# Softmax sums inverted on 128x7 through DRAM, and banks emptied whole, in a fused attention and expert kernel

## The chip, the cores and the metric

The kernel runs on one core of a Trainium2 chip. The metric is the device time of one execution in microseconds, from the profiler's clock; the times of three runs are given by their median.

## The reference

An attention over 2 batches, 12 heads, 448 positions and 64 features per head, with capped scores, feeds two expert blocks that work on 896 tokens of 768 features. The expert weights come as 64-bit floats.

```python
scores = scale * np.matmul(q, k.transpose(0, 1, 3, 2))
scores = cap * np.tanh(scores / cap)
scores = scores - np.max(scores, axis=-1, keepdims=True)
attn = np.exp(scores)
attn = attn / (np.sum(attn, axis=-1, keepdims=True) + 1e-09)
attn_out = np.matmul(attn, v)
x = attn_out.transpose(0, 2, 1, 3).reshape(896, 768)
xn = x / np.sqrt(np.mean(x * x, axis=-1, keepdims=True) + 1e-06) * rms_g
g = xn @ w_gate
x = g * (1.0 / (1.0 + np.exp(-g))) * (xn @ w_val) @ w_out
return ((x @ w1) * (x @ w2) @ w3) @ w_out2
```

## The kernel before, in words

The program has two stages. The **attention** works through 12 pairs of heads (`NP`); features lie on partitions. For a pair the keys are cut into chunks of 128, the last half chunks of the two heads together, which makes 42 groups (`NG`). A group is scores on PE (`scores`, line 440: three matmuls per head, on operands split into a high and a low half), tanh and exp on ACT over two banks at once (lines 448 and 454, into the tile `t`), and the values product on PE (`pv`, line 471), which accumulates a head's bank `po`. There are two `po` banks, one per head of a pair. Each head's values stand beside 64 columns of ones, so a bank holds 64 rows of unnormalized values and 64 rows that all equal the softmax sum.

When a pair's last chunk is accumulated, four steps empty its two banks: for each head `take_sum` (lines 482 and 484) copies the 64 rows of sums plus a small guard into half of the tile `sm`, and `take` (lines 180 and 182) copies the 64 rows of values into the tile `xraw`. Then `invert` takes the reciprocal of `sm` in two steps of 128 x 224 on DVE (line 499), `normalize` multiplies `xraw` by it (line 507, DVE or POOL), `square` (line 518, ACT) and `add_square` (line 525) build the sum of squares for the expert block's norm.

```python
def invert(pr, c):
    def run(e):
        r = sums[pr][:, c * S // 2 : (c + 1) * S // 2]
        e.reciprocal(r, r)
```

Into the attention's gaps on PE goes half of the product of the last two weight matrices (`last_product`, lines 642 to 644), whose result waits in DRAM (`m32`). The 64-bit weights are loaded as raw words (`wraw`), rebuilt on POOL, ACT and DVE (lines 264 to 281) and split in two halves (`wo`, `whl`; lines 180 to 187).

The **expert** stage (`experts`, matmuls at lines 791 to 793) is a list of weight tiles, each used for both batches; the first four tiles run for batch 0 before any runs for batch 1, whose norm comes last (`normalize_x`, lines 315 to 330).

What sets the order of the work is a planner (class `Plan`). Every step is a task with its engines and an assumed duration on each, a rank, the tasks it comes after, and the buffers of fixed rings (`rings`) that it makes and uses. `order` plays the tasks through once, and the program is issued in that order: each engine, SP's queue of DMA issues included, works in its own part of it strictly in order and waits wherever the real times differ from the assumed ones. All DMAs of the program are issued by SP.

## Time and profile before

| what | value |
|---|---|
| median of three runs | 644.07 us (643.78 to 645.33) |
| the profiled execution | 644.65 us |
| its span, first to last instruction | 642.5 us |
| attention, first tanh to last exp | 6.86 to 138.19 us |
| first expert matmul | 159.05 us |

The span is a little shorter than the time of the execution, since the launch and the end lie around it. The page names each engine's share of the whole span; as the two stages differ, the views by stretch say more. PE is the matmul engine (TensorE), PEld its weight loads, DVE VectorE, ACT ScalarE, POOL GpSimd, SP the engine that issues the DMAs.

### The profile page before, as it was taken

Reading aid. Unit: us, or ns where it says so; the run is one execution under the profiler, and the core shown is the slowest. Engines: PE = TensorE matmul, PEld = TensorE weight load, DVE = VectorE, ACT = ScalarE, POOL = GpSimd, SP = SyncE. Lnnn points to the kernel's source line nnn. Section 1 sums busy time; section 2 is a strip of 40 time slices with the busy share of each in tenths; the row PEclk is TensorE's granted clock in tenths of the full one; section 3 lists DMA queues with packets and bytes.
Section 4 is the critical chain, followed back from the end, with each engine's and each line's share of the span. In section 5 each row is a group of like instructions: output and inputs, shape, how many; then the busy total and the mean of one; then the engine's idle time right before and its main releaser. Section 6 shows DMA issues by size and latency. Waiting matters only on the chain.

```text
span 642.5 us, 7766 instructions
## 1 busy us (share of the span) xinstructions
PE 625.0 (97%) x2985; PEld 529.0 (82%) x2985; DVE 390.0 (61%) x474; ACT 277.2 (43%) x383; POOL 162.8 (25%) x161
## 2 busy tenths in 40 slices
PE   6899999999999999999999999999999999999996
PEld 2455556669999999999999999999999999999995
DVE  2898999979867677524765555576565564332300
ACT  6798788965434344223433332233332232121111
POOL 1747532213133344222422222211132221000000
PEclk9899999999999999999999999999999999999999
DMA  8554542325345444225863222333222332224411
GB/s 313 171 201 142 186 142 78 112 73 185 112 153 186 138 141 153 93 71 187 258 211 99 98 99 99 107 129 107 99 99 98 99 118 96 66 65 142 141 46 47
DMA packets 33886, 82.91 MB, mean 129 GB/s; under 512 B 2992, under 2 KB 21040, under 8 KB 33840
## 3 DMA queue, kind: packets, MB, share of 16 engines
q1 hardware_dynamic: 33840, 82.33, 38.4%
q8 instruction: 25, 0.41, 0.3%
q14 instruction: 21, 0.17, 0.1%
HBM read 73.27 MB, written 9.04 MB: 128 GB/s over the span
## 4 chain that ended last, share of the span: by engine, by line
PE 82%; DVE 9%; ACT 5%; issue 2%; POOL 1%; DMA 1%; SPq 0%; ACTq 0%; POOLq 0%; DVEq 0%
PE bank L791 25%; PE bank L793 25%; PE bank L792 25%; PE po L471 3%; DVE sm L499 3%; PE pss L440 2%; ACT t L448 1%; DVE wraw L277 1%; ACT t L454 1%; DVE wraw L281 1%; DVE th L187 1%; PE bank L642 1%; POOL xraw L507 1%; PE bank L644 1%; PE bank L643 1%
## 5 line engine op out<-in xcount | busy, mean ns | idle before, releaser
L273 POOL TENSOR_SCALAR wraw<-wraw 128x768 int32<-128x768 uint32 (+1 forms) x71 | 77.6, 1093 | 195.0 <-DMA wraw<-in_w 85.2
L187 DVE TENSOR_TENSOR whl<-wraw,whl 128x768 fp32r<-128x768 f32 (+1 forms) x80 | 70.1, 876 | 79.5 <-POOL whl L184 65.4
L791 PE MATMUL bank<-xn,whl 128*128 128x448 f32 x288 | 105.6, 367 | 0.5 <-POOL wraw L273 0.5
L792 PE MATMUL bank<-xn,whl 128*128 128x448 f32 x288 | 105.6, 367 | 0.0
L793 PE MATMUL bank<-xn,whl 128*128 128x448 f32 x288 | 105.6, 367 | 0.0
L277 DVE SCALAR_TENSOR_TENSOR wraw<-wraw 128x768 int32<-128x768 int32 (+1 forms) x76 | 70.7, 931 | 48.8 <-POOL wraw L273 43.8
L184 POOL TENSOR_SCALAR whl<-wraw 128x768 fp32r<-128x768 f32 (+1 forms) x47 | 42.4, 902 | 202.0 <-PE bank L793 160.8
L281 DVE SCALAR_TENSOR_TENSOR wraw<-wraw 128x768 int32<-128x768 int32 (+1 forms) x76 | 79.2, 1042 | 1.7
L791 PE MATMUL bank<-u,whl 128*128 128x448 f32 x216 | 79.3, 367 | 0.0
L793 PE MATMUL bank<-u,whl 128*128 128x448 f32 x216 | 79.3, 367 | 0.0
L792 PE MATMUL bank<-u,whl 128*128 128x448 f32 x216 | 79.3, 367 | 0.0
L471 PE MATMUL po<-t,v 128*128 128x448 f32 (+1 forms) x192 | 75.1, 566 | 2.6 <-DVE xraw L182 1.4
L264 ACT ACTIVATE wraw<-wraw 128x768 f32<-128x768 f32 (+1 forms) x59 | 52.1, 882 | 45.8 <-DMA wraw<-in_wgv 16.3
L791 PE MATMUL bank<-y,whl 128*128 128x448 f32 x192 | 70.7, 368 | 0.0
L792 PE MATMUL bank<-y,whl 128*128 128x448 f32 x192 | 70.7, 368 | 0.0
L793 PE MATMUL bank<-y,whl 128*128 128x448 f32 x192 | 70.7, 368 | 0.0
L471 PEld LDWEIGHTS po<-t,v 128*128 128x128 f32 (+1 forms) x192 | 31.5, 192 | 33.5 <-issue 25.4
L791 PEld LDWEIGHTS bank<-xn,whl 128*128 128x128 f32 x288 | 54.1, 188 | 5.7 <-POOL wraw L273 0.8
L793 PEld LDWEIGHTS bank<-xn,whl 128*128 128x128 f32 x288 | 54.1, 188 | 4.9
L792 PEld LDWEIGHTS bank<-xn,whl 128*128 128x128 f32 x288 | 54.1, 188 | 4.7
L180 ACT ACTIVATE whl<-wraw 128x768 fp32r<-128x768 f32 (+1 forms) x33 | 28.3, 858 | 42.2 <-PE bank L793 40.6
L448 ACT ACTIVATE t<-pss,small 128x896 f32<-128x896 f32 x42 | 41.9, 998 | 10.3 <-PE pss L440 8.4
(89 smaller groups left out, 938.8 us busy)
## 6 DMA issues: line engine op xcount, KB each, us to landing
wraw<-in_wgv SPq DMA_DIRECT2D x24, 768.0 KB, 4.4
wraw<-in_w SPq DMA_DIRECT2D x16, 768.0 KB, 4.2
wraw<-in_wdn SPq DMA_DIRECT2D x12, 768.0 KB, 4.2
wraw<-in_w3t SPq DMA_DIRECT2D x16, 512.0 KB, 3.9
wraw<-in_wo SPq DMA_DIRECT2D x8, 768.0 KB, 6.7
m<-mo SPq DMA_DIRECT2D x32, 192.0 KB, 2.7
wraw<-m SPq DMA_DIRECT2D x24, 256.0 KB, 3.2
v<-in_v SPq DMA_DIRECT2D x12, 448.0 KB, 3.8
```

The source lines that it names most:

```text
L180: nc.scalar.activation(out_, in_, AF.Copy)
L184: nc.gpsimd.tensor_scalar(out_, in_, 1.0, 1.0, op0=ALU.mult, op1=ALU.mult)
L187: e.tensor_tensor(lo, raw, r32(hi), op=ALU.subtract)
L264: e.activation(h, h, AF.Copy, scale=2.0**-112)
L273: e.tensor_scalar(l, l.bitcast(U32), 0.876 * 2.0**-29, 0.49, op0=ALU.mult, op1=ALU.add)
L277: e.scalar_tensor_tensor(l, h, 3, l, op0=ALU.logical_shift_left, op1=ALU.bitwise_or)
L281: e.scalar_tensor_tensor(l, h, -(2**31), l, op0=ALU.bitwise_and, op1=ALU.bitwise_or)
L448: e.activation(chunks[g], s[:, :, :S], AF.Tanh, scale=tsc)
L471: e.matmul(pos[2 * p + i][:, :S], vals[p][rows, 6 if c == 3 else 2 * c + i, :], x, start=start, stop=stop)
L791: e.matmul(dst, whi[:, c, :], src(0, g, b), start=(g == 0), stop=False)
L792: e.matmul(dst, whi[:, c, :], src(1, g, b), start=False, stop=False)
L793: e.matmul(dst, wlo[:, c, :], src(0, g, b), start=False, stop=(g == total - 1))
```

## The change

Each `po` bank is emptied by one copy of all 128 rows into a new tile `ev` (a ring of four, two pairs). The second head of a pair now has its ones ahead of its values, so its values come out on partitions 64 to 127, where they are wanted. For the first ten pairs one row of sums of each head goes to DRAM (`keep`, into `total`), comes back as 128 x 7 (`gather`, tile `rs`), gets its guard and its reciprocal on DVE (`invert`), goes out again (`put`, into `rcp`) and comes back spread over 64 partitions per head (`spread`, tile `rb`). For the last two pairs the sums are stacked on 128 partitions and inverted as before (`stack`, `invert_stacked`). `normalize` works on 64 rows of one head at a time, from `ev` into `xraw`. The rings of values (`v`), of exponentials (`t`), raw weights (`raw`) and product copies (`mo`) are one deeper. The planner knows a fixed time to landing for the new transfers (`lands`) and a slack for SP's steps behind other engines; the second half of `wo` lies in a pool that is opened when the attention's is closed. The other branch of the program, for large caps, is not run with these inputs.

```diff
-NRAW, NHL, EARLY = 3, 4, 4
+NRAW, NHL, EARLY = 4, 4, 4
...
+    SLACK = 1.5
...
-                if (self.tasks[j]["on"].keys() == {self.tasks[i]["e"]}) == same:
+                on = self.tasks[j]["on"].keys()
+                if (0 if on == {self.tasks[i]["e"]} else 2 if on == {"SP"} else 1) == for_:
                     missing[j] -= 1
...
-                end = [free[e], free[e] + self.LAG[e]]
+                end = [free[e], free[e] + self.LAG[e], free[e] + self.SLACK]
                 if t["size"]:
                     channel = max(channel, now + 1.5) + t["size"] / self.RATE
-                    end = [channel + 0.5] * 2
+                    end = [channel + 0.5] * 3
+                if t["lands"]:
+                    end = [now + t["lands"]] * 3
...
+    total = dram.tile([HP, 2 * S], F32, name="total")
+    rcp = dram.tile([HP, 2 * S], F32, name="rcp")
...
-        rings = dict(qk=2, th=3, v=3, t=4, sm=2, sq=2, s=2, o=2, m=2, raw=NRAW, hl=NHL, mo=2, sg=4, acc=2)
+        rings = dict(qk=2, th=3, v=4, t=5, ev=4, rs=2, rb=3, sq=2, s=2, o=2, m=2, raw=NRAW, hl=NHL, mo=3, sg=4, acc=2)
...
-            def take_sum(i):
-                def run(e):
-                    pr, j = divmod(i, 2)
+            def take(i):
+
+
+                def run(e):
+                    taken[i] = ring(ap, "ev", [P, S])
+                    half(taken[i], pos[i][:, :S], e)
+
+                return run
+
+            def stack(pr, j):
+                def run(e):
                     if j == 0:
-                        sums[pr] = ring(ap, "sm", [P, S])
-                    s = slice(j * D, (j + 1) * D)
+                        inv_[pr] = ring(ap, "rb", [P, S])
+                    r, at = slice(j * D, (j + 1) * D), slice((1 - j) * D, (2 - j) * D)
                     if e is nc.scalar:
-                        e.activation(sums[pr][s], pos[i][D:, :S], AF.Identity, bias=guard[D:])
+                        e.activation(inv_[pr][r], taken[2 * pr + j][at], AF.Identity, bias=guard[at])
                     else:
-                        e.tensor_scalar(sums[pr][s], pos[i][D:, :S], guard[D:], None, op0=ALU.add)
-
-                return run
-
-            def take(i):
+                        e.tensor_scalar(inv_[pr][r], taken[2 * pr + j][at], guard[at], None, op0=ALU.add)
...
+            def invert_stacked(pr, c):
+                def run(e):
+                    r = inv_[pr][:, c * S // 2 : (c + 1) * S // 2]
+                    e.reciprocal(r, r)
...
+            def keep(pr):
+                def run(e):
+                    for j in range(2):
+                        at = D * (1 - j)
+                        e.dma_start(out=total[pr : pr + 1, j * S : (j + 1) * S], in_=taken[2 * pr + j][at : at + 1])
...
+            def gather(pr):
+                def run(e):
+                    rows_[pr] = ring(ap, "rs", [P, 2 * S // P])
+                    e.dma_start(out=rows_[pr], in_=total[pr].rearrange("(p n) -> p n", p=P))
...
+            def invert(pr):
+                def run(e):
+                    e.tensor_scalar(rows_[pr], rows_[pr], guard, None, op0=ALU.add)
+                    e.reciprocal(rows_[pr], rows_[pr])
...
+            def put(pr):
+                def run(e):
+                    e.dma_start(out=rcp[pr].rearrange("(p n) -> p n", p=P), in_=rows_[pr])
+
...
+            def spread(pr):
+                def run(e):
+                    inv_[pr] = ring(ap, "rb", [P, S])
+                    for j in range(2):
+                        e.dma_start(out=inv_[pr][j * D : (j + 1) * D], in_=rcp[pr : pr + 1, j * S : (j + 1) * S].to_broadcast([D, S]))
...
+            def normalize(i):
                 def run(e):
                     pr, j = divmod(i, 2)
                     b, h = divmod(pr, H // 2)
-                    half(x_tile(b, h)[j * D : (j + 1) * D], pos[i][:D, :S], e)
-
...
-            def invert(pr, c):
-                def run(e):
-                    r = sums[pr][:, c * S // 2 : (c + 1) * S // 2]
-                    e.reciprocal(r, r)
...
-            def normalize(pr):
-                def run(e):
-                    b, h = divmod(pr, H // 2)
-                    x = xraw[b][:, h, :]
-                    e.tensor_tensor(x, x, sums[pr], op=ALU.mult)
+                    r = slice(j * D, (j + 1) * D)
+                    e.tensor_tensor(x_tile(b, h)[r], taken[i][r], inv_[pr][r], op=ALU.mult)
...
+                    ev = [evb[2 * p], evb[2 * p + 1]]
+                    done = [add(dict(ACT=0.57, DVE=0.66), take(2 * p + i), r - 2 + i * 0.01, after=[a], makes=[ev[i]], uses=[both[i]]) for i in range(2)]
+                    if p >= NP - 2:
+                        a = [add(dict(ACT=0.66, DVE=0.66), stack(p, 0), r, after=[done[0]], makes=[rbb[p]], uses=[ev[0]])]
+                        a.append(add(dict(ACT=0.66, DVE=0.66), stack(p, 1), r, after=[done[1], a[0]], uses=[ev[1], rbb[p]]))
+                        inv = [add(("DVE", 1.52), invert_stacked(p, c), r + 0.1 * c, after=a, uses=[rbb[p]]) for c in range(2)]
+                    else:
+                        a = add(("SP", 0.9), keep(p), r - 30, after=done, uses=ev, lands=3.2)
+                        a = add(("SP", 0.45), gather(p), r - 30, after=[a], makes=[rsb[p]], lands=2.8)
+                        a = add(("DVE", 0.35), invert(p), r - 30, after=[a], uses=[rsb[p]])
+                        a = add(("SP", 0.45), put(p), r - 30, after=[a], uses=[rsb[p]], lands=3.0)
+                        inv = [add(("SP", 0.9), spread(p), r - 30, after=[a], makes=[rbb[p]], lands=4.0)]
                     done = []
                     for i in range(2):
-                        done.append(add(dict(ACT=0.66, DVE=0.66), take_sum(2 * p + i), r - 2 + i * 0.01, after=[a] + done[:1],
-                                        makes=[] if i else [smb[p]], uses=[both[i]] + ([smb[p]] if i else [])))
                         new = b not in x_alloc
-                        x = add(dict(ACT=0.57, DVE=0.66), take(2 * p + i), r - 2 + 0.1 + i * 0.01, after=[a] + ([] if new else [x_alloc[b]]),
-                                makes=[xb[b]] if new else [], uses=[both[i]] + ([] if new else [xb[b]]))
+                        x = add(dict(DVE=0.66) if h == 5 else dict(DVE=0.66, POOL=1.3), normalize(2 * p + i), r + 0.3 + 0.01 * i,
+                                after=inv + ([] if new else [x_alloc[b]]), makes=[xb[b]] if new else [], uses=[rbb[p], ev[i]] + ([] if new else [xb[b]]))
                         x_alloc.setdefault(b, x)
                         done.append(x)
-                    inv = [add(("DVE", 1.52), invert(p, c), r + 0.1 * c, after=done, uses=[smb[p]]) for c in range(2)]
-                    a = add(dict(DVE=0.66) if h == 5 else dict(DVE=0.66, POOL=1.3), normalize(p), r + 0.3, after=inv, uses=[smb[p], xb[b]])
-                    every.append(a)
-                    a = add(("ACT", 0.58), square(p), r + 0.4, after=[a], makes=[sqb[p]] if h else [], uses=[xb[b]])
+                    a = add(("ACT", 0.58), square(p), r + 0.4, after=done, makes=[sqb[p]] if h else [], uses=[xb[b]])
                     if h:
                         a = add(dict(DVE=0.66) if h == 5 else dict(DVE=0.66, POOL=1.3), add_square(p), r + 0.5, after=[a, sq_last[b]], uses=[sqb[p]])
                     sq_last[b] = a
...
+                        wo[q] = ring(up() if q else big, "BC"[q], [P, 2, HJ, DM], F32R, "wo")
...
+                                 ready=[done[0][0]] if r else over))
...
-    v = np.concatenate([a["v"].reshape(BH, S, D), np.ones((BH, S, D), np.float32)], axis=2).reshape(BH // 2, 2, S, P)
+    v = a["v"].reshape(BH // 2, 2, S, D)
+    ones = np.ones((BH // 2, S, D), np.float32)
+    v = np.stack([np.concatenate([v[:, 0], ones], axis=2), np.concatenate([ones, v[:, 1]], axis=2)], axis=1)
```

Since the planner decides the order, the built order shows more than the diff. On PE, at the end of the first pair and the start of the second (`pss` is a bank pair of scores, `po` the values product), before and with the change:

```order
5 L471 MATMUL po<-t,v 128x448 x2
6 L440 MATMUL pss<-th 128x448 x6
7 L471 MATMUL po<-t,v 128x448 x2
8 L440 MATMUL pss<-th 128x448 x6
9 L471 MATMUL po<-t,v 128x448 x6
10 L440 MATMUL pss<-th 128x448 x12
11 L471 MATMUL po<-t,v 128x448 x2
```

```order
5 L478 MATMUL po<-t,v 128x448 x2
6 L447 MATMUL pss<-th 128x448 x6
7 L478 MATMUL po<-t,v 128x448 x2
8 L447 MATMUL pss<-th 128x448 x6
9 L478 MATMUL po<-t,v 128x448 x8
10 L447 MATMUL pss<-th 128x448 x18
11 L697 MATMUL bank<-wo,whl 128x384
```

One more values product of the second pair comes ahead of the next scores, and three groups of scores then stand in a row. Further on, 102 matmuls of the last product stand behind the last values product, where 93 did.

On DVE, from the first emptied bank on (`sm` sums, `th` split heads, `ev` emptied banks, `rs` the 128 x 7 sums), before and with the change:

```order
13 L182 COPY xraw<-po 64x448
14 L484 TENSOR_SCALAR sm<-po,small 64x448
15 L277 SCALAR_TENSOR_TENSOR wraw<-wraw 128x768
16 L499 RECIPROCAL sm<-sm 128x224
17 L187 TENSOR_TENSOR th<-qk,th 128x960
18 L499 RECIPROCAL sm<-sm 128x224
19 L187 TENSOR_TENSOR th<-qk,th 128x960
```

```order
13 L188 COPY ev<-po 128x448
14 L283 SCALAR_TENSOR_TENSOR wraw<-wraw 128x768
15 L287 SCALAR_TENSOR_TENSOR wraw<-wraw 128x768
16 L283 SCALAR_TENSOR_TENSOR wraw<-wraw 128x768
17 L287 SCALAR_TENSOR_TENSOR wraw<-wraw 128x768
18 L193 TENSOR_TENSOR th<-qk,th 128x960
19 L283 SCALAR_TENSOR_TENSOR wraw<-wraw 128x512
20 L287 SCALAR_TENSOR_TENSOR wraw<-wraw 128x512
21 L193 TENSOR_TENSOR wo<-wraw,wo 128x768
22 L188 COPY ev<-po 128x448
23 L531 TENSOR_SCALAR rs<-rs,small 128x7
24 L532 RECIPROCAL rs<-rs 128x7
```

The wide reciprocals are gone, weight steps stand in their place, and the first pair's small reciprocal comes after the second pair's first bank copy.

On SP, the transfers of the first two pairs among the loads, with the change, after the first pair's sums have gone out (`total` and `rcp` lie in DRAM, `rb` takes the spread reciprocals):

```order
18 L525 DMA rs<-total 128x7
19 L407 DMA qk<-in_qk 128x960
20 L431 DMA v<-in_v 128x896
21 L257 DMA wraw<-in_w3t 128x1024
22 L516 DMA total<-ev 1x448 x2
23 L538 DMA rcp<-rs 128x7
24 L407 DMA qk<-in_qk 128x960
25 L257 DMA wraw<-in_w3t 128x1024 x2
26 L525 DMA rs<-total 128x7
27 L546 DMA rb<-rcp 64x448 x2
```

Between two steps of one pair stand loads of heads, values and weights, and the steps of the next pair.

## Rows read from the trace of the kernel before

**Rows 1.** The page, busy share (part 1) and granted clock by slice (part 2).

```profile
PE 625.0 (97%) x2985; PEld 529.0 (82%) x2985; DVE 390.0 (61%) x474; ACT 277.2 (43%) x383; POOL 162.8 (25%) x161
...
PEclk9899999999999999999999999999999999999999
```

**Rows 2.** Busy us (count) of PE, PEld, DVE, ACT, POOL by stretch; clock, DMA share, GB/s.

```profile
6.86:137.20 130.34, 124.44 (x523) 70.61 (x522) 113.89 (x121) 112.90 (x135) 55.63 (x52) 0.99 0.46 158
...
159.05:642.50 483.45, 477.34 (x2352) 438.75 (x2352) 255.67 (x324) 151.08 (x229) 100.89 (x97) 1.00 0.36 119
```

**Rows 3.** ACT's groups, 6.86 to 137.2 us: busy, mean ns, idle before.

```profile
L454 ACT ACTIVATE t<-t,small 128x896 f32<-128x896 f32 x42 | 43.7, 1041 | 1.1
L448 ACT ACTIVATE t<-pss,small 128x896 f32<-128x896 f32 x42 | 41.9, 998 | 10.3 <-PE pss L440 8.4 <-PE po L471 1.6
L482 ACT ACTIVATE sm<-po,small 64x448 f32<-64x448 f32 x12 | 7.6, 632 | 0.4
L180 ACT ACTIVATE xraw<-po 64x448 f32<-64x448 f32 x12 | 6.5, 538 | 2.5 <-DVE sm L484 2.3
L518 ACT ACTIVATE sq<-xraw 128x448 f32<-128x448 f32 x8 | 4.6, 575 | 4.9 <-POOL xraw L507 3.1 <-DVE xraw L507 1.7
...
L271 ACT ACTIVATE wraw<-wraw 128x768 int32<-128x768 uint32 (+1 forms) x3 | 2.5, 822 | 0.3 <-DMA wraw<-in_w3t 0.3
...
L180 ACT ACTIVATE mo<-bank 128x384 f32<-128x384 f32 x2 | 0.9, 472 | 0.0
```

**Rows 4.** DVE's groups by shape, 0 to 158 us.

```profile
L499 DVE RECIPROCAL sm<-sm 128x224 f32<-128x224 f32 x24 | 35.7, 1524 | 0.2
...
L484 DVE TENSOR_SCALAR sm<-po,small 64x448 f32<-64x448 f32 x11 | 7.6, 690 | 3.3 <-PE po L471 1.8 <-ACT xraw L180 1.2
...
L182 DVE COPY xraw<-po 64x448 f32<-64x448 f32 x11 | 6.8, 615 | 2.0 <-ACT sm L482 1.8
...
L507 DVE TENSOR_TENSOR xraw<-xraw,sm 128x448 f32<-128x448 f32 x7 | 5.3, 758 | 0.1
...
L200 DVE TENSOR_TENSOR small<-small 128x1 f32<-128x1 f32 x1 | 0.2, 159 | 0.0
```

**Rows 5.** Timeline at the attention's end: start, us, engine, instruction, idle before.

```profile
137.15 1.04 ACT L454 ACTIVATE t<-t,small 128x896 f32<-128x896 f32 x1
...
141.14 0.68 PE L642 MATMUL bank<-wo,whl 128*128 128x384 f32 x1
...
157.70 0.33 PE L644 MATMUL bank<-wo,whl 128*128 128x384 f32 x1
...
158.22 0.34 PE L644 MATMUL bank<-wo,whl 128*128 128x384 f32 x1
159.05 0.44 PE L791 MATMUL bank<-xn,whl 128*128 128x448 f32 x1 [0.49 <-POOL wraw L273]
```

**Rows 6.** POOL's group of line 507, 0 to 158 us.

```profile
L507 POOL TENSOR_TENSOR xraw<-xraw,sm 128x448 f32<-128x448 f32 x5 | 9.3, 1856 | 15.7 <-DVE sm L499 11.8 <-ACT t L448 3.9
```

**Rows 7.** DMA issues up to 150 us (KB, us to landing), then the tile m.

```profile
m<-mo SPq DMA_DIRECT2D x11, 192.0 KB, 1.9
...
small<-in_rg SPq DMA_DIRECT2D x1, 3.0 KB, 5.5
...
L613 SPq DMA_DIRECT2D m<-mo x32: 319/320/931, 71.5 to 326.0; - x32
...
DMA to landing us min/median/max: 1.8/3.1/4.7
```

**Rows 8.** The tile sm: min/median/max ns, first and last start.

```profile
L482 ACT ACTIVATE sm<-po,small x13: 629/632/635, 19.0 to 140.9; 64x448 f32<-64x448 f32 x13
```

**Rows 9.** Who PE waited for: total us, times, longest.

```profile
PE po L471 <- DVE xraw L182: 1.4, 2, 0.8
```

**Rows 10.** Busy time by stretch, two stretches near the start.

```profile
21.60:24.00 2.40, 2.40 (x5) 1.15 (x6) 2.40 (x3) 2.40 (x3) 1.41 (x1) 0.79 0.53 214
24.00:27.00 3.00, 3.00 (x6) 1.31 (x5) 3.00 (x3) 1.43 (x2) 0.75 (x1) 0.60 0.43 111
```

More of the change, by code (lines that the diff above doesn't have):

```diff
@@ L70, in buf, with add @@
         return b
-    def add(self, engines, run, rank, after=(), makes=(), uses=(), size=0, behind=()):
+    def add(self, engines, run, rank, after=(), makes=(), uses=(), size=0, behind=(), lands=0):
         if not isinstance(engines, dict):
@@ L81, in add @@
         self.tasks.append(
-            dict(on=engines, run=run, rank=rank, after=[x for x in after if x is not None], makes=list(makes), held=held, size=size, behind=list(behind))
+            dict(on=engines, run=run, rank=rank, after=[x for x in after if x is not None], makes=list(makes), held=held, size=size, behind=list(behind), lands=lands)
         )
@@ L142, in order @@
                 todo -= 1
-                ends += [(end[0], i, True), (end[1], i, False)]
+                ends += [(x, i, k) for k, x in enumerate(end)]
                 moved = True
@@ L152, in order @@
                 finish(*x[1:])
-                if not x[2]:
+                if x[2] == 1:
                     for h in self.tasks[x[1]]["held"]:
@@ L375, in attend @@
             NP = BH // 2
-            raws, heads, vals, chunks, pos, sums, sqs = {}, {}, {}, {}, {}, {}, {}
+            raws, heads, vals, chunks, pos, taken, rows_, inv_, sqs = {}, {}, {}, {}, {}, {}, {}, {}, {}
             qkb, thb = {p: buf("qk") for p in range(1, NP)}, {p: buf("th") for p in range(NP)}
             vb, tb, ob = {p: buf("v") for p in range(NP)}, {g: buf("t") for g in range(NG)}, {i: buf("o") for i in range(BH)}
-            smb, sqb = {p: buf("sm") for p in range(NP)}, {p: buf("sq") for p in range(NP)}
+            evb, rsb = {i: buf("ev") for i in range(BH)}, {p: buf("rs") for p in range(NP)}
+            rbb, sqb = {p: buf("rb") for p in range(NP)}, {p: buf("sq") for p in range(NP)}
             first_of = lambda p: 7 * (p // 2) + 3 * (p % 2)
@@ L585, in layer, with prep_wo @@
         wo_done, wob = {}, [buf("B", -1), buf("C", -1)]
-        def prep_wo(q, rank, when, step):
+        def prep_wo(q, rank, when, step, over=()):
             done = wo_done[q] = []
@@ L704, in attend_any @@
                 for k in range(NK):
-                    nc.tensor.matmul(po, tv[:, order[k], :D], pt[:, k, :], start=(k == 0), stop=(k == NK - 1))
+                    nc.tensor.matmul(po, tv[:, order[k], rows], pt[:, k, :], start=(k == 0), stop=(k == NK - 1))
                 x = x_tile(b, h)
@@ L738, in experts @@
             at = [t[0] for t in seq].index("prod")
-            prep_wo(1, 2000 + 10 * (at - 8.5), 60 + at - 8.5, 2)
+            prep_wo(1, 2000 + 10 * (at - 8.5), 60 + at - 8.5, 2, over)
             def get_w(k):
```

11 lines of the change are left out of this document (7 added, 4 removed).

## The prediction

> **What bounds the kernel now.** Start with the page: PE is busy in 97% of the span and its granted clock is full in nearly every slice [rows 1], which reads like a kernel that nothing off PE can help. That figure is an average over two different stages, so the next view is busy time by stretch [rows 2]. From 159.05 us on the expert layers run: PE is busy 477 of 483 us, DVE 256, ACT 151, and the change issues the same matmuls there. Nothing is to be had in that stage. In the attention, from the first tanh at 6.86 us to the last one's stretch at 137.2, the other engines are nearly full too: of 130.3 us DVE is busy 113.9, ACT 112.9, POOL 55.6. PE shows 124.4, but a modelled end covers the start of a wait, so this is not PE at its peak.
>
> Who sets the pace in the attention? Every chunk goes scores (PE), tanh, exp (ACT), values product (PE). ACT's groups [rows 3] say what it does in those 130 us: 84 tanh and exp are 85.6 us, which nobody can take from it; the banks' emptying (sums 7.6, values 6.5) is 14.1. Its idle time is mostly waits for PE's scores (8.4), which in turn stand behind bank waits on PE, and 2.3 in front of L180, which waits for DVE's half of the same emptying. DVE's groups [rows 4] show where the time goes that the change aims at: 24 reciprocals of 1.52 us are 35.7 us. The end of the attention is in the timeline [rows 5]: last exp from 137.15 to 138.19, last values product done before 141.14, then 93 matmuls of the second product and the sums' matmul up to 158.22, then the experts. So whatever ends the last exp earlier moves the whole expert stage, less what PE still has to do in between.
>
> **The change, part by part.** *ACT up to the last exp*, counted in the built order. Twelve sums go (12 x 0.632 = -7.6 us); twelve value copies of 64 rows become ten bank copies of 128 rows by 448, at the same 448 elements per partition and so at the same 0.538 (-1.1); one square less (-0.6), two product copies go to DVE (-0.9), one weight step goes and two come (+0.8 at 0.82 each) [rows 3]. Sum: -9.4 us.
>
> *DVE.* Away: 20 of 24 reciprocals (-30.5), 11 sums (-7.6), 11 copies (-6.8), 7 normalizings (-5.3). Added: 12 bank copies at 0.615 (+7.4), 17 normalizings of 64 x 448 at the old mean of 0.758 (+12.9), twenty steps on 128 x 7, nearest to the 128 x 1 steps at 0.16 (+3.2), some 3 for additions and copies that move over [rows 4]. Net about -24 us of 114. DVE does not set the end, so I give this nothing directly; it is the cover under the next two items.
>
> *POOL* normalizes 7 times instead of 5. Each took 1.856 us [rows 6], against DVE's mean of 0.758, and ACT's squares wait behind it: 3.1 us for five [rows 3]. Two more: +1.2 us of waiting on ACT.
>
> *Waits.* The wait of 2.3 in front of ACT's L180 goes, since a bank now has one reader that waits for PE alone. New waits come: DVE stops in order at the small reciprocal (for the gathered row) and at the normalizing (for the spread one), and behind it stand the next pair's head split (L187), weight steps and bank copies. The trace of before has no such wait. Below, the cost can be nothing: DVE has 16 us idle already and 24 more, over ten pairs 2.4 us each beyond what it has. Above it is the 11 us of the first rival. I take 2.3, the wait that they replace, because the transfers' nearest row is close to its short end (below). The two entries cancel.
>
> *The transfers.* Ten pairs make six each, 60 in all, with four landings in a row: sums out, gathered, reciprocals out, spread. The nearest ones are the stores `m<-mo`: 1.9 us median to landing in the attention, 1.8 to 4.7 over the run, 0.32 of SP to issue [rows 7]. At 1.9 the path from the emptied bank is 2.2 + 2.2 + 0.3 + 2.2 + 2.5 and two normalizings at 0.61, 10.7 us. The banks' copies have a ring of four, so pair p+2 may overwrite when pair p is normalized. Pairs end 11.1 us apart (19.0 to 140.9 in eleven steps [rows 8]), so there are some 20.8 us: 10 in hand. The Trainium skill, page "DMA: Bandwidth & Descriptors", section "Anatomy of one DMA", puts a fixed 2.0 us on every transfer, which is about the shortest row here; by it the path would be an estimated 11 us and the sum the same. The same page's "Specifications" says that pieces under 512 B are read, modified and written; the 28-byte pieces of the gather and the put fall under that, and no row here shows its price: the one load in such pieces, the 24 bytes per partition of `in_rg`, landed after 5.5 us but behind five larger ones [rows 7]. SP spends 60 x 0.32 = 19 us more of 130 on issuing; it mostly waits for buffers there, so nothing. But each transfer waits in SP's order, and the loads of heads, values and weights stand behind it; their rings are one deeper (`v`, `raw`), which is the cover.
>
> *PE's order.* Nine matmuls of the second product move behind the last values product: 102 instead of 93. Three take 0.52 us [rows 5]: +1.6 us. The second half of `wo` now lies in memory that the attention frees; its loads stood behind the attention in SP's order before too, and its use comes after eighteen weight tiles, so nothing.
>
> *Last two pairs* keep two reciprocals each, and stack their sums first with one more 64-row step (0.69). Behind them PE has 102 matmuls (17.7 us) and the first tiles of batch 0, so nothing.
>
> **Sum:** -9.4 + 1.2 - 2.3 + 2.3 + 1.6 = -6.6 us. The profiled execution took 644.65 us (span 642.5), 0.6 over the median of 644.07, so 638.0 in its terms and **637.4 us** against the runs' median. A difference of 0.3%, 1.9 us, is what a measurement of this kernel can tell from none.
>
> **The rivals.**
>
> *1. The transfers come late: slower.* At the longest landing seen, 4.7 us, the path is 4 x 4.7 + 5 x 0.32 + 0.3 + 1.2 = 21.9 us against 20.8 in hand. Then the copy of pair p+2 waits 1.1 us for a buffer, PE waits for the bank, and it repeats in each of the ten pairs from the third on: 11 us, 648.4. It decides from a mean landing of about 4.4 us. For it: 768 KB loads share the queue, and SP's order puts hops behind waits for other buffers. Against it: the median of 1.9. Chance 0.14.
>
> *2. ACT's freed time turns into waiting for PE.* Half of the 8.4 us that tanh waits for scores comes back on top and half of the 9.4 is lost: the gain shrinks to 1 to 3 us, 641 to 643. For it: tanh waits for PE even now, with PE shown as busy 124 of 130 us. Against it: some of PE's own waits are for banks that are still being emptied, 1.4 us of its visible gaps behind DVE's copies alone [rows 9]. Chance 0.18.
>
> *3. More than the sum.* After the bank waits near 20 us PE's clock fell: it was granted 0.79 and 0.60 of full speed between 21.6 and 27 [rows 10], a stretch partly at the lower of its two levels (1.2 of 2.4 GHz), and ACT idled behind it. A bank emptied by two engines at once (0.62 instead of four steps in two lines) may keep PE busy enough. At 0.79 and 0.60 that stretch lost 0.5 + 1.2 = 1.7 us; with the bank waits of later pairs and half of tanh's waits, 3 to 6 us more than the sum: 631.5 to 634.5. Chance 0.18.
>
> *4. The change doesn't do what it says.* In the built order the small reciprocals stand where a wide pair stood, and no pair but the last two has a wide one; I give this nothing.
>
> **How the numbers follow.** The forecast band, 634.5 to 640.5, has the remaining 0.50. The range must leave out 2 in 10 at most: it starts at 631, below rival 3, and ends at 645.5, which takes in rival 2 and leaves out most of rival 1. Faster means under 642.1: 0.50 + 0.18 + about half of rival 2, 0.77 with rounding down for what I have not thought of: 0.75. Slower means over 646.0: most of rival 1, 0.13. The rest, 0.12, is within 0.3%.
>
> **What would show it.** Right: DVE's busy time up to the last exp about 24 us lower, ACT's about 9; the last exp near 130 us and the first expert matmul near 152; the stretch from there to the end still 483 us long; landings of the small transfers under 3 us. The first rival would show as bank copies (`ev<-po`) or po matmuls that wait behind a normalizing, and as landings over 4 us; the second as an ACT idle sum before tanh above 10 us; the third as a clock of 1.00 around 24 us. The prediction is wrong if the last exp does not move by 5 us or more, or if the expert stage grows because its first weights come later than the attention ends.

## The result: slower, and the profile after

| what | before | after |
|---|---|---|
| median, runs side by side | 644.7 us (643.78 to 646.99) | 654.15 us (651.74 to 656.45) |
| ratio, 95% interval | | 1.0141 [1.0095, 1.0187] |
| the profiled execution, its span | 644.65, 642.5 us | 651.74, 649.8 us |
| last exp ends | 138.19 us | 141.37 us |
| first expert matmul | 159.05 us | 164.56 us |

The forecast was 637.4 us. The profiled execution is the fastest of the four with the change: it lies 7.1 us above the one profiled before, where the medians lie 9.4 us apart, so the trace shows most of the loss and not all. Between the two spans are 7.3 us: 5.5 are lost before the first expert matmul and 1.8 behind it. The page's busy line and clock line first; then busy time by stretch, with columns as in [rows 2]. [rows 2] ends where the last exp starts; the first stretch here ends with it, so its counterpart of before, to the same mark, stands ahead of it:

```profile
PE 626.8 (96%) x2985; PEld 529.8 (82%) x2985; DVE 374.8 (58%) x481; ACT 268.3 (41%) x371; POOL 165.4 (25%) x158
...
PEclk9999799999999999999999999999999999999998
```

```profile
6.86:138.19 131.33, 125.43 (x526) 71.07 (x525) 114.88 (x122) 113.89 (x136) 55.63 (x52) 0.99 0.45 157
...
6.86:141.37 134.51, 124.08 (x513) 69.68 (x511) 96.10 (x124) 102.91 (x119) 59.70 (x51) 0.96 0.53 174
164.56:649.84 485.28, 477.54 (x2353) 438.54 (x2352) 259.48 (x329) 153.97 (x233) 99.49 (x95) 1.00 0.35 117
```

Work left DVE and ACT: 18.8 and 11.0 us less up to the last exp, where about 24 and 9.4 were forecast. Yet the stretch is 3.2 us longer, and PE issued 513 matmuls in it where it had issued 526. Engines that got lighter and a stage that got longer: so the reader looks for waits. ACT's groups up to the last exp (against [rows 3]):

```profile
L461 ACT ACTIVATE t<-t,small 128x896 f32<-128x896 f32 x42 | 43.7, 1042 | 1.1
L455 ACT ACTIVATE t<-pss,small 128x896 f32<-128x896 f32 x42 | 42.0, 999 | 14.8 <-PE pss L447 14.8
L186 ACT ACTIVATE ev<-po 128x448 f32<-128x448 f32 x10 | 5.2, 529 | 0.0
L566 ACT ACTIVATE sq<-xraw 128x448 f32<-128x448 f32 x7 | 4.0, 572 | 5.8 <-POOL xraw L555 3.4 <-DVE xraw L555 2.4
...
L186 ACT ACTIVATE whl<-wraw 128x512 fp32r<-128x512 f32 x2 | 1.4, 676 | 9.0 <-DVE wraw L287 9.0
```

The bank copies are as cheap as forecast, and their wait is gone (2.5 to 0.0). But the idle time ahead of tanh grew from 10.3 to 14.8, and two weight steps wait 9.0 us for DVE: together more than the 11.0 us that ACT was freed of. DVE by shape, 0 to 165 us (against [rows 4]):

```profile
L193 DVE TENSOR_TENSOR th<-qk,th 128x960 fp32r<-128x960 f32 x11 | 14.9, 1356 | 5.7 <-ACT th L186 5.6
L555 DVE TENSOR_TENSOR xraw<-ev,rb 64x448 f32<-64x448 f32 x17 | 12.2, 716 | 5.0 <-DMA rb<-rcp 4.7
...
L531 DVE TENSOR_SCALAR rs<-rs,small 128x7 f32<-128x7 f32 x10 | 3.9, 393 | 10.5 <-DMA rs<-total 10.5
...
L532 DVE RECIPROCAL rs<-rs 128x7 f32<-128x7 f32 x10 | 2.0, 201 | 0.3
```

Two things stand there. DVE waits 15.2 us for the transfers (10.5 for gathered, 4.7 for spread rows). And the head split, eleven times in both kernels, takes 14.9 us; before it took this:

```profile
L187 DVE TENSOR_TENSOR th<-qk,th 128x960 fp32r<-128x960 f32 x11 | 12.7, 1154 | 5.6 <-ACT th L180 5.6
```

Who let PE wait, in the view of PE's waits (total, times, longest):

```profile
PE po L478 <- DVE ev L188: 4.4, 2, 4.1
PE pss L447 <- ACT t L455: 3.4, 1, 3.4
```

The longest wait of each can be followed in the timeline (start, us, engine, line, instruction, idle before). The first, near 30 us:

```profile
28.30 1.35 DVE L287 SCALAR_TENSOR_TENSOR wraw<-wraw 128x512 int32<-128x512 int32 x1
29.08 1.31 POOL L272 TENSOR_SCALAR wraw<-wraw 128x768 f32<-128x768 f32 x1
29.57 1.62 DVE L193 TENSOR_TENSOR wo<-wraw,wo 128x768 fp32r<-128x768 f32 x1
29.68 0.66 ACT L186 ACTIVATE whl<-wraw 128x512 fp32r<-128x512 f32 x1 [5.55 <-DVE wraw L287]
30.25 0.52 ACT L186 ACTIVATE ev<-po 128x448 f32<-128x448 f32 x1
30.68 0.99 ACT L455 ACTIVATE t<-pss,small 128x896 f32<-128x896 f32 x1
...
31.72 1.34 PE L447 MATMUL pss<-th 64*128 64x448 f32 x6 [3.40 <-ACT t L455]
```

DVE's weight steps run late, beside POOL's. ACT, in its order, stands 5.55 us in front of a step that needs their result, while a full bank and a tanh are queued behind it; PE stops 3.40 us for the tanh. No transfer has a part in it. The second, near 70 us:

```profile
65.36 0.54 SPq L257 DMA_DIRECT2D wraw<-in_w3t  x1
...
66.01 0.37 SPq L525 DMA_DIRECT2D rs<-total  x1
...
71.19 0.49 DVE L531 TENSOR_SCALAR rs<-rs,small 128x7 f32<-128x7 f32 x1 [3.18 <-DMA rs<-total]
...
71.72 0.20 DVE L532 RECIPROCAL rs<-rs 128x7 f32<-128x7 f32 x1
71.83 1.12 DVE L188 COPY ev<-po 128x448 f32<-128x448 f32 x2
...
72.47 2.39 PE L478 MATMUL po<-t,v 64*128 64x448 f32 x4 [4.07 <-DVE ev L188]
```

Here it is the transfer: the gather is issued 0.65 us behind a 512 KB load, and DVE's step for it starts 5.2 us later, after a wait of 3.18. Two bank copies stand behind that step and PE waits 4.07 us for them. After it, PE's granted clock falls: 0.83 over 60 to 80 us (it was 1.00 there before), a stretch partly at the lower of its two levels; the four values matmuls that follow take 2.39 us. Behind the first wait it had fallen too, to 0.60 over 31.7 to 36.0 us.

```profile
60.00:80.00 20.00, 15.93 (x55) 8.04 (x53) 15.29 (x22) 11.23 (x12) 9.96 (x10) 0.83 0.52 165
```

One more reading, of DVE and POOL side by side. Four lines with the change, then two of before:

```profile
42.42 1.12 DVE L193 TENSOR_TENSOR th<-qk,th 128x960 fp32r<-128x960 f32 x1
42.51 2.05 POOL L555 TENSOR_TENSOR xraw<-ev,rb 64x448 f32<-64x448 f32 x1 [3.57 <-PE pss L447]
...
86.12 1.29 POOL L272 TENSOR_SCALAR wraw<-wraw 128x768 f32<-128x768 f32 x1
86.56 1.86 DVE L193 TENSOR_TENSOR th<-qk,th 128x960 fp32r<-128x960 f32 x1
```

```profile
26.02 1.09 DVE L187 TENSOR_TENSOR th<-qk,th 128x960 fp32r<-128x960 f32 x1
26.25 1.86 POOL L507 TENSOR_TENSOR xraw<-xraw,sm 128x448 f32<-128x448 f32 x1 [3.23 <-DVE sm L499]
```

The same split takes 1.86 us in one place and 1.12 in another, with POOL beside it in both. What tells them apart is which began first. With the change four of the eleven splits took 1.60 to 1.86 us, and in each of them a step of POOL had begun 0.44 to 0.64 us earlier and was still running. The seven others took 1.12 to 1.16, two of them with POOL beside them for 92% and 81% of their time: there POOL's step began after the split, and POOL's was the long one (2.05 us at 42.51, where the same step took 1.13 at 69.45). The planner assumes 1.2 for the split. Before, the order was mostly the other way round: all five of POOL's normalizings began 0.23 us behind a split and took 1.86 us, the splits 1.09, and only one split met a running step of POOL (1.60 us).

Bank copies, whose one large input lies in a bank of PE's, took 0.585 to 0.626 with POOL or without. The wide reciprocals that the change removed took 1.48 to 1.57 us each, with POOL beside them for up to 98% of their time or not at all; what the change put in their place has two inputs in memory. Summed from the starts and ends in the two traces, up to the last exp, such steps of DVE (splits, weight steps, normalizings, additions) took 69.6 us before, 31.5 of them beside POOL, and 81.2 with the change, 42.5 of them beside POOL.

### The profile page after: what moved, and what is told of

Read it like the earlier page. It is cut to its first block, busy times and chain, and to the rows that moved or that the text cites. A ratio compares the mean times of both kernels' runs of the same rounds, so it can differ in the third digit from the quotient of the medians.

```text
span 649.8 us, 7867 instructions
## 1 busy us (share of the span) xinstructions
PE 626.8 (96%) x2985; PEld 529.8 (82%) x2985; DVE 374.8 (58%) x481; ACT 268.3 (41%) x371; POOL 165.4 (25%) x158
## 4 chain that ended last, share of the span: by engine, by line
PE 87%; DMA 4%; DVE 4%; issue 1%; ACT 1%; SPq 1%; DVEq 0%; ACTq 0%
PE bank L846 24%; PE bank L847 24%; PE bank L848 24%; PE po L478 7%; PE pss L447 3%; DMA rs<-total 2%; DMA wraw<-in_wgv 1%; PE bank L697 1%; DVE th L193 1%; DVE wraw L283 1%; PE bank L699 1%; PE bank L698 1%; DMA qk<-in_qk 1%; DMA v<-in_v 1%; DVE wraw L287 0%
## 5 line engine op out<-in xcount | busy, mean ns | idle before, releaser
L279 POOL TENSOR_SCALAR wraw<-wraw 128x768 int32<-128x768 uint32 (+1 forms) x67 | 76.2, 1137 | 178.4 <-DMA wraw<-in_w 82.2
L193 DVE TENSOR_TENSOR whl<-wraw,whl 128x768 fp32r<-128x768 f32 (+1 forms) x80 | 71.9, 899 | 73.1 <-POOL whl L190 57.3
L283 DVE SCALAR_TENSOR_TENSOR wraw<-wraw 128x768 int32<-128x768 int32 (+1 forms) x76 | 72.7, 957 | 54.5 <-POOL wraw L279 47.8
L478 PE MATMUL po<-t,v 128*128 128x448 f32 (+1 forms) x192 | 76.8, 581 | 6.3 <-DVE ev L188 4.4
L287 DVE SCALAR_TENSOR_TENSOR wraw<-wraw 128x768 int32<-128x768 int32 (+1 forms) x76 | 79.4, 1045 | 1.5
L270 ACT ACTIVATE wraw<-wraw 128x768 f32<-128x768 f32 (+1 forms) x55 | 48.6, 885 | 42.9 <-DMA wraw<-in_wgv 20.1
L186 ACT ACTIVATE whl<-wraw 128x768 fp32r<-128x768 f32 (+1 forms) x36 | 30.6, 850 | 57.2 <-PE bank L848 46.9
L455 ACT ACTIVATE t<-pss,small 128x896 f32<-128x896 f32 x42 | 42.0, 999 | 14.8 <-PE pss L447 14.8
```

Of the source, the lines that this page charges most:

```text
L186: nc.scalar.activation(out_, in_, AF.Copy)
L193: e.tensor_tensor(lo, raw, r32(hi), op=ALU.subtract)
L270: e.activation(h, h, AF.Copy, scale=2.0**-112)
L279: e.tensor_scalar(l, l.bitcast(U32), 0.876 * 2.0**-29, 0.49, op0=ALU.mult, op1=ALU.add)
L283: e.scalar_tensor_tensor(l, h, 3, l, op0=ALU.logical_shift_left, op1=ALU.bitwise_or)
L287: e.scalar_tensor_tensor(l, h, -(2**31), l, op0=ALU.bitwise_and, op1=ALU.bitwise_or)
```

## The experiments

Fifteen kernels were run beside the two. Marks are read from each profile: the end of the last exp, and the start of the first expert matmul.

| run | median us | ratio to before, 95% | last exp | first expert |
|---|---|---|---|---|
| after | 654.15 | 1.0141 [1.0095, 1.0187] | 141.4 | 164.6 |
| e1_stack_all | 652.66 | 1.0124 [1.0088, 1.0160] | 136.3 | 165.0 |
| e2_lands | 654.54 | 1.0151 [1.0111, 1.0190] | 153.0 | 150.2 |
| e3_no_chain | 648.26 | 1.0053 [1.0032, 1.0075] | 132.1 | 162.8 |
| e4_rings_only | 647.72 | 1.0041 [1.0021, 1.0061] | 139.7 | 161.8 |
| h1_costs | 643.30 | 0.9967 [0.9947, 0.9988] | 132.7 | 155.1 |
| h2_costs_queue | 653.85 | 1.0134 [1.0088, 1.0181] | 155.1 | 143.6 |
| h3_costs_nochain | 638.63 | 0.9900 [0.9853, 0.9947] | 121.8 | 152.3 |
| h4_before_costs | 642.46 | 0.9967 [0.9940, 0.9994] | 130.0 | 157.1 |
| i1_stack_costs | 650.13 | 1.0075 [1.0047, 1.0103] | 126.3 | 163.1 |
| i2_ev6 | 638.56 | 0.9914 [0.9884, 0.9943] | 125.7 | 150.0 |
| i3_act | 653.86 | 1.0148 [1.0115, 1.0181] | 143.4 | 166.7 |
| i5_ev6_h1 | 640.96 | 0.9945 [0.9926, 0.9964] | 128.1 | 153.6 |
| j1_ev6_only | 646.07 | 1.0006 [0.9988, 1.0025] | 132.0 | 159.4 |
| j2_ev6_lands | 644.41 | 1.0001 [0.9984, 1.0017] | 135.3 | 158.6 |
| j3_stack_ev6 | 652.77 | 1.0111 [1.0073, 1.0148] | 125.1 | 166.5 |

**Parts of the change: e1 to e4.** Every pair stacked, no transfers:

```diff
-                    if p >= NP - 2:
+                    if True:
```

> All twelve pairs invert their sums as the last two do (stacked, 128x224 twice on DVE); no transfers. Theory L (late transfers hold DVE's queue, and with it the bank copies): the waits of DVE for rs and rb, 15 us, go, but 30 us of reciprocals come back on DVE, so about the time of before, 642 to 647. Theory C (weight steps of DVE and POOL that now run side by side slow each other, and ACT waits behind DVE): 30 us of reciprocals return on a DVE that is slowed as well, 652 or more. Theory R (the deeper rings and the moved half of wo spoil the order): 650 or more, as with the change.

652.7 us: still slow without a transfer, so the transfers alone are not the cause. Next, the planner told that each hop takes 5.0 or 5.5 us (the first of the four lines is shown; the others go from 2.8, 3.0 and 4.0 to 5.0, 5.0 and 5.5):

```diff
-                        a = add(("SP", 0.9), keep(p), r - 30, after=done, uses=ev, lands=3.2)
+                        a = add(("SP", 0.9), keep(p), r - 30, after=done, uses=ev, lands=5.0)
...
```

> Only the planner's times to landing are raised, to 5.0, 5.0, 5.0 and 5.5 us; the transfers are the same. Theory L: the small reciprocals and the normalizings stand later in DVE's and POOL's order, bank copies no longer wait behind them; DVE's wait for rs falls from 10.5 us to under 4, and the time to 640 to 647. If the path is simply too long for the ring of four bank copies, it stays over 650 with PE waiting for banks. Theory C: 648 to 655, since the contention is the same.

654.5 us, lost in another place. In this plan the attention is spread out until 153 us and the experts' first tiles run before it ends; the last norm then comes late, and PE waits for it:

```profile
170.24 0.62 DVE L573 TENSOR_TENSOR acc<-acc,sq 128x448 f32<-128x448 f32 x1 [0.64 <-ACT sq L566]
...
170.92 1.86 PE L321 MATMUL bank<-acc,ones 128*128 128x448 f32 x2 [7.48 <-DVE acc L573]
```

The first ten pairs multiplied by a tile of ones, their sums left out, so that neither transfers nor small reciprocals remain:

```diff
-                    e.tensor_tensor(x_tile(b, h)[r], taken[i][r], inv_[pr][r], op=ALU.mult)
+                    e.tensor_tensor(x_tile(b, h)[r], taken[i][r], (inv_[pr] if pr >= NP - 2 else unit)[r], op=ALU.mult)
...
+                        inv = done
```

> The first ten pairs make no transfers and no reciprocal, and normalize by a constant tile of ones: the sums of those pairs are left out of the result. Theory L: without any of these waits the forecast's gain appears, 632 to 639. Theory C: DVE and POOL still do the weight steps side by side, so 645 to 652. Theory R: over 648.

648.3 us: slower than before although it does less. PE's waits:

```profile
PE po L480 <- ACT t L463: 4.7, 1, 4.7
PE po L480 <- DVE ev L189: 4.6, 1, 4.6
```

In the first ACT stood 3.8 us in front of a square for POOL's normalizing; in the second a bank copy stood behind a split of 1.60 us and two weight steps of 1.62 and 1.47. The deeper rings of `v`, `t`, `raw`, `mo` and the moved half of `wo`, put into the kernel before:

```diff
-NRAW, NHL, EARLY = 3, 4, 4
+NRAW, NHL, EARLY = 4, 4, 4
...
-        rings = dict(qk=2, th=3, v=3, t=4, sm=2, sq=2, s=2, o=2, m=2, raw=NRAW, hl=NHL, mo=2, sg=4, acc=2)
+        rings = dict(qk=2, th=3, v=4, t=5, sm=2, sq=2, s=2, o=2, m=2, raw=NRAW, hl=NHL, mo=3, sg=4, acc=2)
...
```

> The kernel before with the deeper rings and the moved half of wo alone. Theories L and C: the time of before within 0.5%, 641 to 647. Theory R: 649 or more.

647.7 us, between the two ranges expected: a small loss (0.41%), not the 9.4.

**The planner's durations: h1 to h4.** Only assumed durations change here. The steps are the same; the planner issues them in another order and gives a few to another engine (up to the first expert matmul POOL has 60 where it had 63, ACT 144 where it had 138):

```diff
-            two = 0.17 + N / 960
-            unary = dict(POOL=0.25 + N / 1000, ACT=0.2 + N / 1200)
+            two = 1.3 * (0.17 + N / 960)
+            unary = dict(POOL=1.25 * (0.25 + N / 1000), ACT=0.2 + N / 1200)
...
-                a = add(dict(ACT=1.0, POOL=1.3), first, r, after=[a], makes=[thb[p]], uses=[qkb[p]])
-                h_done[p] = [add(("DVE", 1.2), second, r, after=[a], uses=[qkb[p], thb[p]])]
+                a = add(dict(ACT=1.0, POOL=1.5), first, r, after=[a], makes=[thb[p]], uses=[qkb[p]])
+                h_done[p] = [add(("DVE", 1.45), second, r, after=[a], uses=[qkb[p], thb[p]])]
...
```

Normalizing goes from 0.66 to 0.8 on DVE and from 1.3 to 1.75 on POOL, the addition of squares from 0.66 to 0.8 on DVE.

> The change with only the planner's durations raised to what the traces show when DVE and POOL work side by side (two-operand weight steps on DVE x1.3, weight steps on POOL x1.25, head split 1.45, normalizing 0.8 on DVE and 1.75 on POOL). Same instructions, other order. Theory C (DVE's two-operand steps and POOL's steps slow each other, the reciprocals did not, and the planner's order breaks on it): ACT and PE no longer wait behind late DVE steps, 643 to 648. Theory L (late transfers alone): the waits for rs and rb stay, 649 to 656. Theory P (any new order loses, since it was tuned): 649 to 656 too.

643.3 us, 10.9 below the changed kernel. DVE still waits 8.4 us for gathered rows, but PE's waits have shrunk, and of DVE's two-input steps only 31.7 us lie beside POOL up to the last exp, as before the change:

```profile
PE pss L447 <- ACT t L455: 2.5, 3, 1.5
PE bank L699 <- DVE whl L193: 1.7, 1, 1.7
```

The same with landings that follow the planned load on the queue (`max(now + lands, channel + 2.2)`):

> As h1, and the planner also lets a small transfer land no sooner than 2.2 us after what is already in the queue. Theories L and C both at work: the best of these with transfers, 638 to 645, with DVE's waits for rs under 3 us and no wait of PE over 2 us. L alone: 640 to 647 and as good as it would be without the durations. Theory P: 650 or more.

653.9 us, a miss: it was to be the best with transfers, and only the reading that any new order loses named 650 or more. Again the last exp is at 155 us, and PE waits 5.2 us for the late norm. e3's edit (sums of ten pairs left out) with h1's durations:

> As e3_no_chain (ten pairs normalized by ones, no transfers, the sums of those pairs left out), with the raised durations. Theory C: the two long waits of PE of e3, 4.7 and 4.6 us, and the low clock behind them go; 636 to 643 against e3's 648. If something else than the durations holds it: 646 to 650.

638.6 us, 9.6 below e3. Against h1 the transfers and their small steps, with the order that they bring, cost 4.7 us. And the kernel before with h1's durations:

> The kernel before with the raised durations. Theory C says that before is limited by the reciprocals on DVE and its order was near right: 643 to 647. Theory P: 649 or more, as its order changes as well.

642.5 us, 0.33% faster: before, the plan was less wrong. With these durations in both, the change is worth nothing (643.3 and 642.5).

**Rings, landings, and a control: i1 to i5.** e1 with h1's durations:

> Every pair stacked and inverted by two wide reciprocals, no transfers (as in e1_stack_all), planned with the longer durations of DVE's and POOL's steps. Theory C (what slows the changed kernel is a plan whose durations are too short once DVE and POOL run side by side): 652.7 us falls to 641 to 645, about where the kernel before stands with the same durations (642.5), since the work of the other engines is then much the same; no PE wait of the attention over 2.5 us after 25 us. Rival W (whole-bank emptying itself, with two more 64-row steps per pair, is dear): 648 or more, with DVE busy over 115 us up to the last exp.

A miss: 650.1 us. The rival, that whole-bank emptying with two more 64-row steps per pair is dear, named 648 or more, but with DVE busy over 115 us up to the last exp; it was busy 106.9. The last exp is 12 us earlier than before and the first expert matmul 4 us later. At one place the weights of the last product were not ready, since DVE was busy:

```profile
149.17 0.69 PE L699 MATMUL bank<-wo,whl 128*128 128x384 f32 x1 [3.91 <-DVE whl L193]
```

h1 with more bank copies and longer landings:

```diff
-NRAW, NHL, EARLY = 4, 4, 4
+NRAW, NHL, EARLY = 3, 4, 4
...
-        rings = dict(qk=2, th=3, v=4, t=5, ev=4, rs=2, rb=3, ...
+        rings = dict(qk=2, th=3, v=4, t=5, ev=6, rs=3, rb=4, ...
...
```

The landings go from 3.2, 2.8, 3.0 and 4.0 us to 4.2, 4.2, 4.2 and 5.0.

> Changed kernel, longer durations, transfers planned to land after 4.2, 4.2, 4.2 and 5.0 us, and six bank copies, three gathered rows and four spread tiles in place of four, two and three, with one buffer less of raw weights to make room. Theory D (the long planned landings failed in e2_lands and h2_costs_queue because a ring of four bank copies then set the pace of the whole plan): with six the last exp is back under 135 us and the time is 639 to 643, with DVE waiting under 4 us for gathered rows. Rival (long landings push the last batch's norm behind the attention whatever the ring): last exp after 145 us and 650 or more.

638.6 us, faster than both kernels. In it DVE waits for gathered rows twice, and the clock is full:

```profile
DVE rs L531 <- DMA rs<-total: 2.4, 2, 2.2
```

```profile
6.86:125.69 118.83, 115.88 (x506) 65.59 (x503) 90.20 (x119) 105.67 (x126) 47.26 (x43) 1.00 0.58 190
```

The control, only ACT's weight steps planned 1.25 times as long (the emptying steps, which the expectation names too, keep their durations):

```diff
-            unary = dict(POOL=0.25 + N / 1000, ACT=0.2 + N / 1200)
+            unary = dict(POOL=0.25 + N / 1000, ACT=1.25 * (0.2 + N / 1200))
```

> Control: the changed kernel with one planned duration altered that was right, ACT's emptying and splitting steps by 1.25. Theory C (right durations of DVE and POOL are what helps): no gain, 650 to 656 us. Rival P (any other order has a chance to be good, and h1_costs was a lucky draw): below 647 would speak for it.

653.9 us: this other order does not help. It stays closer to the changed kernel's than h1's does, so it is one weak control. And i2's rings with the old landings:

> As i2_ev6, but with the landings planned as in the changed kernel (3.2, 2.8, 3.0, 4.0), so that only the rings differ from h1_costs. Theory C and D: close to h1_costs, 641 to 645 us, with DVE's waits for gathered rows still 6 to 10 us. If these waits and not the rings are what the transfers cost, i2_ev6 is faster than this one by 2 us or more; if the two are within 1 us, the waits cost nothing.

641.0 us, with 12.5 us of DVE's waits for gathered rows:

```profile
DVE rs L531 <- DMA rs<-total: 12.5, 6, 4.2
```

So ten more microseconds of DVE's waiting go with 2.4 us more, and the two intervals overlap.

**What does it alone: j1 to j3.** i2's rings on the changed kernel (six bank copies, three gathered rows, four spread tiles, one raw buffer less), without and with i2's landings, the durations as in the changed kernel:

> The changed kernel's durations and landings, with six bank copies, three gathered rows, four spread tiles and one raw buffer less. Theory C (the short durations are a cause by themselves): in the first pairs the same steps of DVE and POOL still come late, 648 us or more, with a PE wait over 2 us before 80 us. Rival R (the ring of four bank copies was the cause): 645 or less.

> As j1_ev6_only, with landings planned at 4.2, 4.2, 4.2 and 5.0 us; it differs from i2_ev6 (638.6 us) in the durations alone. Theory C: 645 us or more, 7 or more over i2_ev6. Rival R: within 3 us of i2_ev6.

646.1 and 644.4 us: neither reading holds alone. The four rings together, with no duration touched, take 8.1 us off the changed kernel; which of them does it was not tried. One wait of PE of 4.0 us for a bank copy stays in j1 all the same, behind a small step that waits for its gather, and the clock is 0.83 over 40 to 60 us there. j2 is 5.9 above i2, less than the 7 forecast, and that is what the durations are worth with these rings and landings.

Six pairs of these runs differ in the raised durations alone, and in each the one with the raised durations is faster: 10.9 us (changed kernel and h1), 9.6 (e3, h3), 5.9 (j2, i2), 5.1 (j1, i5), 2.5 (e1, i1, whose intervals overlap) and 2.5 (before and h4). That speaks against a lucky draw more than the control does. Last, i2 with wide reciprocals for every pair, no transfers:

> As i2_ev6, with every pair stacked and inverted wide, without transfers; only the landings are planned as in the changed kernel, which here matter to no step. If the transfers' relief of DVE is worth the 6 us that i2_ev6 gains on the kernel before, this one stands 4 us or more above i2_ev6, at 643 or more, with DVE busy 10 us or more longer up to the last exp. If rings and durations make the gain and the transfers nothing: within 2 us of i2_ev6.

652.8 us, 14.2 above i2, with the last exp at the same place (125.1 and 125.7). The difference is what else was done until then:

```profile
6.86:125.08 118.22, 112.86 (x463) 59.43 (x460) 105.03 (x109) 110.57 (x133) 46.29 (x41) 0.99 0.41 145
```

DVE is busy 105.0 us against i2's 90.2, and PE has issued 463 matmuls against 506. The 43 that are missing are nearly all of the last product; they stand behind the attention, and there PE waits for their weights and results:

```profile
149.16 0.44 PE L699 MATMUL bank<-wo,whl 128*128 128x384 f32 x1 [3.31 <-DVE whl L193]
166.54 0.47 PE L846 MATMUL bank<-xn,whl 128*128 128x448 f32 x1 [3.38 <-ACT mo L186]
```

## Why the prediction was wrong

**What held.** The sizes of ACT's work: 11.0 us less busy time against a forecast of 9.4. The wait of 2.3 in front of the emptying on ACT went. The expert stage was nearly untouched (483.5 to 485.3). Rival 4 fell: the wide pair is gone in all pairs but two. POOL normalized 7 times, but ACT's idle time before squares grew by 2.8 us and not 1.2 (4.9 to 5.8, and 1.9 before the two first squares, which had not waited). The 1.856 us on which that term rests was not the price of a normalizing alone: each of the five lay behind a split of DVE, and the seven with the change took 1.40 on average, on half the rows.

**The step that failed first: "DVE does not set the end, so I give this nothing directly; it is the cover under the next two items."** DVE became lighter, by 18.8 us up to the last exp and not 24. But a mean of free time covers nothing at the moment when the queue is late. The planner put 11 us more of DVE's two-input steps beside POOL's, at durations that hold for each alone; real ones were up to 1.86 against a planned 1.2. ACT and PE then waited in order: ACT 9.0 us for two weight steps, PE 3.40 us behind one of them. The Trainium skill, page "SBUF — State Buffer", section "SBUF: two separate sides", has a rule for it: DVE and GpSimd share a pair of ports, held by the instruction that starts first until it ends, and a DVE step with two inputs in SBUF needs it against a GpSimd step that reads SBUF. The trace agrees: 1.60 to 1.86 us for a split that met a running step of POOL, 1.12 to 1.16 for one that began first, and no change for a copy out of a bank.

That the plan's durations cost the time is shown by h1: new durations alone took off 10.9 us, the control i3 0.3, and five other pairs go the same way. That the lengthened steps beside POOL are what made the old durations wrong is read from the traces; no run took POOL away. And the durations are not the only way out: the rings of j1 take off 8.1 us without them.

**The second: the term of +2.3 us for new waits.** DVE waited 15.2 us for the transfers. The forecast took the value near a landing of 1.9 us, that of stores that nothing depended on. DVE waited for six of the ten gathers, and these took 2.3 to 5.2 us from issue to use, 3.6 on average; the two longest, 4.9 and 5.2, make 7.9 of its 10.5 us. The figure of the Trainium skill by which the forecast checks its 1.9 us, page "DMA: Bandwidth & Descriptors", section "Anatomy of one DMA", is given there for transfers that GpSimd issues; these are SP's, and the runs decide. Under a plan with better durations the chain costs 4.7 us (h1 against h3).

Rival 1 had the direction right, and its landing of over 4.4 us only for the two longest gathers. Its mechanism was another: no copy waits for a buffer in each of ten pairs. What the trace shows instead is one wait of 4.07 us for a bank copy that stands in DVE's order behind a small step, and the fall of the clock after it. That this one wait makes the loss is not shown: j1 has the same kind of wait, 4.0 us long, with the same 0.83 behind it, and is 8.1 us faster. The longest of DVE's waits for a gather, the 4.70 us up to 42.04, stopped PE not at all: PE is busy all through it. Longer planned landings failed with four bank copies (e2, h2) and work with i2's rings.

Rival 2, that ACT's freed time turns into waiting, came closer than its chance of 0.18 says: the 11.0 us that ACT was freed of came back as idle time, but for the most part in front of DVE's late results (9.0) and less in front of PE's scores (4.5). Its sign, over 10 us idle before tanh, was met by the row of before already. Rival 3's sign was there too, a clock of 1.00 from 21.6 to 27 us; the fall only came later, behind the two waits.

**The third: the sum was made on the wrong engine.** "Whatever ends the last exp earlier moves the whole expert stage, less what PE still has to do": the second half was priced at 1.6 us and is the greater one. i1, i2 and j3 end their last exp within 1.3 us of each other and start the experts at 163.1, 150.0 and 166.5. In every kernel of this list but e2 and h2 the same 633 matmuls stand ahead of the first expert's (a window can catch one more), so what moves that mark shows as PE's idle time and its clock. Before, changed, i2 and j3, from 0 to the mark, columns as in [rows 2]:

```profile
0.00:159.05 159.05, 147.70 (x633) 90.20 (x634) 134.34 (x151) 126.07 (x155) 61.95 (x64) 0.99 0.47 161
...
0.00:164.56 164.56, 149.22 (x634) 91.28 (x635) 115.36 (x153) 114.36 (x138) 65.94 (x63) 0.97 0.52 172
...
0.00:149.95 149.95, 141.91 (x633) 88.57 (x634) 106.83 (x146) 117.45 (x146) 52.17 (x54) 1.00 0.55 179
...
0.00:166.54 166.54, 148.47 (x634) 91.01 (x634) 139.86 (x160) 132.49 (x170) 53.02 (x55) 0.98 0.43 149
```

PE stands idle 11.4, 15.3, 8.0 and 18.1 us in them, and the clock takes an estimated 1.6, 4.9, 0 and 3.3 us (the missing hundredths times the stretch). From before to the change that is 4.0 and 3.3 us more, and the mark moved by 5.5; from i2 to j3 it is 10.0 and 3.3, and the mark lies 16.6 later; what is left lies in PE's busy time, whose ends are modelled. The last product is what PE can do in the gaps of the attention, and DVE has a part in preparing its weights. There DVE's relief is worth its price: 14.2 us between j3 and i2.

So i2 stands 6.3 us below the 644.87 of before measured beside it, and that this is close to the -6.6 of the forecast is luck. The raised durations alone take 2.5 us off the kernel before (h4), which leaves 3.4 to 3.9 for the change with i2's rings and landings; and i2 gains 9.1 us ahead of the experts and gives back 3.6 in their stage (487.1 against 483.5). As built the change loses its gain to a plan that does not know its own steps. Open is which of the durations and which of the rings matter most, how much of i1's and j3's loss is the plan's tail rather than DVE's load, and why i2's expert stage is longer. Neither the planner's new slack for SP's steps, which stands in every kernel but before, e4 and h4, nor the whole-bank emptying in the old order was run alone.

## What to carry to other kernels

Where a table of durations sets the order, a change of what runs beside what makes it wrong; measure the steps again in the new neighbourhood before the change is judged. Price a change on the engine that must be fed until the next stage, by how much of its work is done at the mark, and not only by when the last step of another engine ends. Free time on an in-order engine covers a wait only if nothing urgent is queued behind the waiting step.

## What was not expected of the hardware

A DVE step with two inputs in memory took up to 1.6 times as long when it met a running step of POOL (1.86 against 1.15 us), and where it began first POOL's step was the long one (2.05 against 1.13), while copies out of a bank kept their 0.6 us. An addition on 128 x 7 took 0.22 to 0.23 us in six of ten pairs; the other four ran beside POOL and took 0.31 to 1.16, which makes the mean of 0.39. A reciprocal on 128 x 7 took 0.20. The two long waits of PE in the attention (3.40 and 4.07 us) were followed by a stretch of lower clock (0.60 over 4.3 us, 0.83 over 20), so that a wait cost more than its own length.
